# Loads of q, k and v in pieces of two pairs, tail groups inside one PSUM tile, the last output in two halves, and a new instruction order: a linear-attention and channel-mix kernel

## Chip, cores, metric

One core of a Trainium2 chip. The metric is device time in microseconds (us). The kernel is tuned already: every engine's instruction stream is written out by hand in one long list of words, and each engine works its own words off in that order. The question is what a change of loads, buffers and order does to it.

## The reference

```python
def phi(x):                                   # x: (8, 8, 576, 64), w_phi: (64, 128)
    proj = np.einsum('bhsd,df->bhsf', x, w_phi)
    proj = proj - np.max(np.abs(proj), axis=-1, keepdims=True)
    return np.concatenate([np.exp(proj), np.exp(-proj)], axis=-1)
q_p, k_p = phi(q), phi(k)
kv = np.einsum('bhsf,bhsd->bhfd', k_p, v);  z = np.sum(k_p, axis=2)
attn = einsum('bhsf,bhfd->bhsd', q_p, kv) / (einsum('bhsf,bhf->bhs', q_p, z)[..., None] + 1e-06)
x = attn.transpose(0, 2, 1, 3).reshape(8, 576, 512)
x_prev = x shifted by one position
xk = mu_k * x + (1 - mu_k) * x_prev;   xr = mu_r * x + (1 - mu_r) * x_prev
k = np.maximum(xk @ w_k, 0.0)                 # 512 -> 1024
out = sigmoid(xr @ w_r) * (k * k @ w_v)       # 1024 -> 512
```

Eight batches, each of 8 heads taken as 4 pairs (32 pairs n = 0 to 31). Each pair's 576 positions are 512 (the main part) and 64 (the "tail"). The tails of a batch are worked as a group. Then come two matmul stages of the feed-forward part per batch, on the tiles named ps_h, ps_r and ps_v.

## The kernel before

The order is a list of words. `name:slot` gives the PSUM slot, `/ENGINE` the engine, `+n@s` dummy matmuls that fill a wait, `.d` the end of a transfer. A number without a dot is a pair, `4.0` is batch 4 from its pair 0 on, `7.2` batch 7 from its pair 2 on: `lk7.2` loads k there, `mh18` splits the maxima of pair 18. An excerpt at pair 7 of 31, with five loads in a row:

```text
mt7:1 mc7/ACT lk3.0 lq3.0 lv3.0 lk4.0 lq4.0 rq8 lk4.0.d:0 kc6/ACT r0.1:0 th0.1 ka7 ea7 eb7 ...
```

A load is one transfer per tensor and batch (1152 KB in fp32, cast on the way to 576 KB in bf16; the sizes below, as in the profile, are those in bf16), issued by POOL. From batch 2 on there is one for all four pairs:

```python
def ld(which):
    def f():
        t = get(nat, b, inp, [128, NP, 2 * X], BF, "nat")
        src, o = ((k, 0), (q, X))[which]
        nc.gpsimd.dma_start(out=t[:, a0:a1, o:o + X], in_=heads(src, b, a0, a1))
    return f
def ldv():
    t = get(vt, b, inp, [128, NP, X], BF, "vt")
    nc.gpsimd.dma_start(out=t[:, a0:a1, :], in_=heads(v, b, a0, a1))
...
lparts = {b: [(0, NP)] for b in range(B)}
lparts[0] = [(0, 1), (1, 2), (2, 4)]
lparts[1] = [(0, 2), (2, 4)]
```

PSUM is used as three tiles of two banks (`P0` to `P2`) and two of one bank (`M0`, `M1`). A tail group takes one P tile and, one after the other, two M tiles:

```python
def tp():    # projections of the tails: k in bank 0, q in bank 1 (for its maxima)
    s["ps"] = ps = ptile(A, "ps_e")
    ...
def mhe():   # maxima split in two bf16 parts, on POOL
    ... nc.gpsimd.tensor_copy(...); nc.gpsimd.tensor_tensor(..., op=ALU.subtract)
def mte():   # transpose of the maxima
    s["pm"] = pm = motile(("mo", "m" + tag), "ps_me")
    nc.tensor.transpose(pm[:, 0:64].bitcast(BF), mh, ident)
def kae():   # subtracts the maxima from k's half: bank 0 of ps_e
def ekt():   # two exponentials on ACT that read bank 0 of ps_e (tiles tk0, tk1)
def qte():   # q again, transposed and less its maxima
    s["pq"] = ps = motile(("mo", "q" + tag), "ps_qe")
def eqe():   # two exponentials on ACT that read ps_qe (tiles tq)
```

The query exponentials of a pair, and the mix of x with its neighbour:

```python
def eq(pn):
    t = s[f"q{pn}"] = mid.tile([128, 2, 512], BF, name=f"q{pn}", bufs=BUFS["qpn"])
    for h in range(2):
        nc.scalar.activation(t[:, h, :]..., s["qT"]...[:, h], AF.Exp, scale=...)
def mix(i):                # xk, xr: one DVE instruction each
    nc.vector.scalar_tensor_tensor(out=t[...], in0=s["d"], scalar=mu[:, a:a + 1],
                                   in1=xs[:, a, 0:S], op0=ALU.mult, op1=ALU.add)
def mhx():                 # split of a pair's maxima, on POOL: tiles mhl
BUFS = {... "kpn": 2, "qpn": 2, "krelu": 3, "rt": 3, "kvs": 2, "d": 2, ...}
```

Of the kernel before, what the change touches and what calls it, by code (L numbers as in the profile page):

```python
# [19 lines left out]
ones ident lv0.0 lv0.0.d:0 lk0.1 lq0.1 lv0.1 dve2 hk hq hk.d:0 lk0.1.d:0 dve3 hq.d:0 lk0.0.d/ACT  # L20
lq0.0.d/DVE lk0.2 lq0.2 pt0:2+9@0 wphi wphi.d:0 mus dve1 lv0.2 lk1.0 pb0/DVE pa0/ACT tr0 tp0.0:2+1@0
rt0.0 mhe0.0 lk0.2.d:0 qp0:1 rq0 lq0.2.d:0 kp0:0 rk0 mte0.0:1+3@0 lq1.0 lq1.0.d:0 lv1.0 mh0
lq0.1.d:0 pt1:1 pa1/DVE mce0.0/ACT kae0.0 lk1.2 lq1.2 lv1.2 pb1/ACT tr1 lq1.2.d:0 qp1:1+2@0 mt0:1
rq1 ekt0.0 mc0/ACT wk.0 pt2:2 ka0 pb2/DVE pa2/ACT kp1:1 rk1 mh1 ea0 pt3:2 pb3/ACT lk1.0.d:0 eb0
pa3/DVE tr3 mt1:1+4@0 mc1/DVE tr2 vc0/POOL wk.1 qp2:2 ka1 ea1 mus.d:0 eb1 rq2 kv0:0 kc0/DVE wr.0
wk.1.d:0 wr.1 lv1.2.d:0 kp2:2+1@0 rk2 wv.0 qt0:0 pt4:1+1@0 lv1.0.d:0 mh2 mt2:1+1@0 qa0 qb0 lk1.2.d:0
pa4/DVE pb4/DVE qte0.0:0 eqe0.0 tp0.1:1 mc2/DVE ka2 tr4 lv0.2.d:0 pt5:0 ea2 rt0.1 mhe0.1
mte0.1:0+1@1 pb5/DVE wv.0.d:0 pa5/DVE eb2 mce0.1/DVE kae0.1+2@1 lv0.1.d:0 ekt0.1 pt6:0 pb6/ACT
pa6/DVE pt7:2 pa7/DVE nd0:1 qt1:0 rd0 pb7/ACT vc1/POOL vc2/POOL vc3/ACT qp3:2 rq3 kp3:1+1@1 wv.1 rk3
mh3 tr6 qa1 qb1 tp0.2:2+3@1 qte0.1:0 tr7 eqe0.1 rt0.2 mhe0.2 kv1:0 kc1/ACT xt0:1 xf0/ACT mt3:0  # L30
mc3/ACT nd1:0 tr5 vc4/POOL xe0/ACT ka3 ea3 eb3 df0/POOL mte0.2:1+1@0 rd1 xt1:0 mce0.2/DVE kae0.2
ekt0.2 tp1.0:0 qte0.2:1 eqe0.2 rt1.0 qp4:1 qt2:2 lk2.0 qa2 qb2 mhe1.0 mte1.0:1 rq4 xa0 kv2:1 kc2/ACT
mce1.0/DVE kae1.0 ekt1.0 vc5/POOL xf1/DVE xb0 qte1.0:1 wr.0.d:0 kp4:2 kv3:1 eqe1.0 kc3/ACT nd2:0 rk4
mh4 mt4:1 rd2 qp5:1 mc4/ACT ka4 rq5 xe1/ACT wk.0.d:0 ea4 eb4 lq2.0 xt2:1 lq2.0.d:0 qp6:0 rq6
df1/POOL xa1 qt3:1+1@0 qa3 kv4:2+1@0 kc4/DVE wk.d xb1 wr.1.d:0 kp5:0 qt4:2+1@0 rk5 qb3 nd3:1 rd3 mh5
xe2/ACT mt5:0+3@0 lk2.0.d:0 tr2.0 xf2/ACT xt3:1 qa4 qb4 mc5/ACT df2/DVE ka5 xe3/ACT xf3/ACT tr2.2
xa2 xb2 wv.1.d:0 ea5 eb5 nd4:2 rd4 df3/POOL xa3 qt5:1 qa5 xb3 kv5:0+3@0 tr2.2.d:0 kp6:2 xt4:1
xf4/ACT xe4/DVE kc5/ACT h0.0:0 h0.1:1 qb5 rl0.0/ACT rl0.1/ACT sq0.0/ACT vc6/POOL vc7/DVE rk6 qp7:1
nd5:0 df4/POOL rq7 mh6 mt6:1 mc6/ACT h0.2:0 rl0.2/ACT qt6:1 qa6 xa4 tr2.0.d:0 wr.d r0.0:1 tr9 xb4
sq0.2/POOL th0.0 tr8 rd5 h0.3:0 qb6 sq0.1/POOL rl0.3/DVE lv2.0 lv2.0.d:0 xt5:1 xf5/DVE xe5/DVE ka6  # L40
kp7:0 h0.4:0 h0.5:1 qp8:1 ea6 df5/POOL eb6 rl0.4/ACT sq0.4/ACT rk7 mh7 sq0.3/ACT kv6:2 rl0.5/DVE
mt7:1 mc7/ACT lk3.0 lq3.0 lv3.0 lk4.0 lq4.0 rq8 lk4.0.d:0 kc6/ACT r0.1:0 th0.1 ka7 ea7 eb7 tr11 tr10
lq3.0.d:0 tp2.0:1 rt2.0 h0.6:1 r0.2:0 rl0.6/DVE sq0.6/ACT th0.2 nd6:2 rd6 h0.7:1 mhe2.0 mte2.0:0
mce2.0/DVE vc8/POOL vc9/POOL kv7:0 kc7/DVE rl0.7/ACT vc10/POOL kae2.0 ekt2.0 qp9:2 rq9 qte2.0:1
xt6:0 sq0.7/POOL qt7:0 lk3.0.d:0 xf6/DVE xe6/DVE eqe2.0 qa7 qb7 kp8:1 rk8 kp9:2 rk9 wv.d sq0.5/POOL
v0.0:0 ob0.0 tr3.0 so0.0 mh8 mt8:1 nd7:0 mc8/ACT ka8 mh9 mt9:0 mc9/ACT xa5 tr3.2 xb5 v0.1:1 rd7
ob0.1 tr3.2.d:0 vc11/ACT ea8 df6/POOL eb8 xa6 xb6 v0.2:0 ob0.2 xt7:1 xe7/ACT xf7/ACT qt8:1 qa8 qb8
df7/DVE xa7 xb7 ka9 lv3.0.d:0 vc12/POOL kv8:0 r0.3:0 tr3.0.d:0 tr13 tr12 lq4.0.d:0 th0.3 v0.3:1
kc8/DVE ob0.3 kp10:0 so0.1 qp10:1 rq10 rk10 ea9 eb9 h1.0:0 h1.1:1 rl1.0/ACT sq1.0/ACT nd8:1 rd8
kv9:2 kc9/ACT h1.2:0 qt9:1 qp11:2 mh10 rq11 rl1.1/ACT xz8 rl1.2/ACT sq1.2/POOL mt10:1 so0.2 mc10/ACT  # L50
sq1.1/POOL h1.3:0 rl1.3/DVE qa9 qb9 r1.0:1 th1.0 sq1.3/POOL kp11:2 rk11 mh11 ka10 ea10 h1.4:0 tr15
eb10 lv4.0 rl1.4/DVE sq1.4/ACT h1.5:1 rl1.5/DVE mt11:0 mc11/DVE so0.3 nd9:1 qp12:0 sq1.5/ACT ka11
xz8.d:0 ea11 eb11 h1.6:0 h1.7:1 vc13/POOL vc14/POOL tr14 vc15/POOL rd9 rq12 xz9 qt10:1 xz9.d:0
rl1.7/DVE rl1.6/DVE lk5.0 kv10:2 kc10/DVE tp3.0:0 sq1.7/POOL rt3.0 qa10 mhe3.0 qb10 r1.1:1 th1.1
he0.0:0 rle0.0/DVE nd10:1 r1.2:1 sq1.6/ACT mte3.0:0 mce3.0/ACT rd10 xz10 xz10.d:0 qt11:2 th1.2
kp12:1 xu8/POOL df8/DVE xa8 so0.0.d:0 kae3.0 xu9/POOL qa11 qb11 rk12 v1.0:1 ob1.0 mh12 ekt3.0
he0.1:0 mt12:1 mc12/ACT xb8 kv11:2 lv4.0.d:0 so0.1.d:0 tr4.0 df9/DVE rle0.1/ACT kc11/ACT qp13:0
qte3.0:1 sqe0.0/DVE eqe3.0 xu10/POOL df10/POOL ka12 kp13:2 so0.2.d:0 so0.3.d:0 so1.0 ea12 so1.0.d:0
r1.3:0 eb12 rq13 rk13 nd11:0 rd11 th1.3 v1.1:1 xz11 xz11.d:0 mh13 sqe0.1/ACT xa9 xb9 ob1.1 xa10 xb10
mt13:0 mc13/ACT kv12:0 kc12/ACT ka13 ea13 eb13 qt12:1 qa12 tr4.0.d:0 tr16 vc16/POOL xu11/POOL  # L60
df11/POOL qp14:0 rq14 v1.2:1 ob1.2 qb12 re0:0 the0 kp14:0 rk14 xa11 kv13:2 kc13/DVE so1.1 qt13:1
mh14 xb11 v1.3:0 tr4.2 tr4.2.d:0 tr19 vc17/POOL ob1.3 so1.3 mt14:1 qa13 nd12:2 qb13 mc14/ACT
vc18/POOL qp15:1 rq15 ka14 so1.1.d:0 ea14 so1.2 eb14 lq5.0 rd12 xz12 xz12.d:0 h2.0:0 rl2.0/DVE ve0:1
qt14:2 lq5.0.d:0 obe0 soe0 soe0.d:0 kp15:0 kv14:1 sq2.0/ACT qa14 qb14 lv5.0 lv5.0.d:0 vc19/DVE
h2.1:1 rk15 kc14/ACT h2.2:0 nd13:2 rd13 xz13 xz13.d:0 lk6.0 rl2.1/ACT sq2.1/POOL mh15 rl2.2/ACT
sq2.2/POOL r2.0:1 th2.0 tr18 h2.3:0 so1.3.d:0 mt15:1 tr17 qp16:2 qp17:1 mc15/DVE rl2.3/ACT lq6.0
lv6.0 ka15 ea15 eb15 h2.4:0 h2.5:1 rq16 rq17 sq2.3/POOL rl2.4/ACT xu12/POOL df12/POOL qt15:2 qa15
tp4.0:0 kv15:1 kc15/ACT h2.6:0 sq2.4/ACT rl2.5/DVE rt4.0 mhe4.0 rl2.6/DVE nd14:1 rd14 h2.7:1 qb15
vc20/POOL xa12 sq2.5/POOL lk5.0.d:0 xu13/POOL mte4.0:0 kp16:2 rk16 mce4.0/ACT kp17:1 rk17 kae4.0
mh16 rl2.7/ACT ekt4.0 r2.1:0 r2.2:1 th2.1 mt16:0 mc16/DVE xb12 xz14 df13/DVE nd15:0 so1.2.d:0 rd15  # L70
sq2.6/ACT xz15 sq2.7/ACT lq6.0.d:0 th2.2 mh17 ka16 ea16 xa13 v2.0:0 ob2.0 xb13 tr5.0 tr5.2 tr5.0.d:0
tr20 v2.1:1 eb16 mt17:0 mc17/ACT xz14.d:0 kv16:2 kc16/ACT ob2.1 vc21/POOL vc22/POOL qp18:0 rq18 ka17
ea17 qte4.0:1 xu14/POOL eb17 kp18:2 rk18 v2.2:0 eqe4.0 tr5.2.d:0 tr23 qp19:1 lk6.0.d:0 xz15.d:0
xu15/POOL df14/POOL xa14 qt16:0 qa16 ob2.2 r2.3:1 th2.3 mh18 v2.3:0 rq19 qb16 df15/POOL mt18:1
mc18/ACT kv17:1 so2.0 kc17/ACT xb14 ka18 ea18 eb18 qt17:0 qa17 qb17 nd16:1 xa15 xb15 h3.0:1 ob2.3
rd16 xz16 h3.1:0 rl3.0/DVE sq3.0/POOL so2.3 qp20:1 kp19:2 h3.2:1 rl3.2/ACT so2.2 rl3.1/DVE rk19
so2.2.d:0 r3.0:0 rq20 h3.3:1 th3.0 mh19 sq3.1/ACT sq3.2/POOL vc23/ACT rl3.3/ACT mt19:0 mc19/DVE
nd17:1 r3.1:0 th3.1 sq3.3/ACT so2.0.d:0 tr22 qt18:0 rd17 xz17 xz17.d:0 xz16.d:0 xu16/POOL qa18 qb18
ka19 ea19 df16/POOL xa16 kv18:1 kc18/DVE h3.4:0 rl3.4/DVE lk7.0 tr21 tp5.0:1 rt5.0 h3.5:1 sq3.4/DVE
rl3.5/ACT h3.6:0 rl3.6/DVE eb19 nd18:0 rd18 h3.7:1 mhe5.0 mte5.0:0 xz18 rl3.7/DVE sq3.5/ACT qt19:2  # L80
qp21:0 xu17/POOL rq21 mce5.0/ACT kae5.0 ekt5.0 sq3.6/POOL df17/POOL r3.2:1 th3.2 qte5.0:0 kv19:1
lv6.0.d:0 eqe5.0 kc19/ACT kp20:0 so2.3.d:0 xb16 he1.0:1 sq3.7/DVE v3.0:0 so2.1 xz18.d:0 so2.1.d:0
tr6.0 rk20 mh20 rle1.0/DVE qa19 qb19 xu18/POOL df18/POOL vc24/POOL mt20:1 mc20/DVE kp21:2 ka20
vc25/POOL ob3.0 so3.0 rk21 mh21 he1.1:1 rle1.1/DVE nd19:1 r3.3:0 rd19 xz19 xz19.d:0 mt21:1 ea20 eb20
xa18 qt20:0 mc21/ACT th3.3 qp22:1 xb18 qa20 lq7.0 rq22 ka21 v3.1:0 v3.2:1 ob3.1 kv20:1 qb20 xa17
xb17 ea21 eb21 so3.0.d:0 kc20/ACT ob3.2 so3.2 qt21:2 kv21:0 kp22:1 tr6.2 so3.1 re1:1 tr6.2.d:0
xu19/POOL df19/DVE xa19 sqe1.0/ACT xb19 tr27 rk22 mh22 v3.3:0 ob3.3 kc21/ACT nd20:0 rd20 sqe1.1/POOL
xz20 qa21 qb21 nd21:2 mt22:0 the1 tr6.0.d:0 h4.0:1 tr24 mc22/ACT ka22 ea22 rd21 qt22:0 so3.2.d:0
qa22 rl4.0/DVE ve1:0 eb22 vc26/POOL sq4.0/DVE lv7.0 r4.0:1 th4.0 tr25 obe1 qb22 so3.3 qp23:2 rq23
vc27/POOL xz21 kp23:1 rk23 h4.1:0 rl4.1/ACT xz20.d:0 h4.2:1 rl4.2/ACT h4.3:0 qp24:0 kv22:2 xz21.d:0  # L90
# [67 lines left out]
def kernel(  # L158
# [17 lines left out]
    nc = tc.nc  # L176
# [351 lines left out]



    XPE = 8
    xkt, xrt = {}, {}

    def add_pair(n):
# [437 lines left out]
```

## Time and profile before

| | before |
|---|---|
| median of 3 runs (later, with the changed kernel, 4 runs) | 305.72 us (305.18) |
| lowest to highest | 304.64 to 307.18 us |
| profiled execution | 304.2 us |
| TensorE busy / idle | 278.4 / 25.8 us |
| first ps_h matmul (end of the start) | 51.9 us |
| DVE, ACT, POOL busy | 240.3, 223.3, 127.4 us |

The prediction below shows the lines behind most of this. Two more are needed for the comparison. The first, from the slices of the page, is the clock that TensorE was granted, in tenths of full speed, in 40 equal slices (9 is 0.9 or more); the second, from the groups, holds the query exponentials: line, engine, operation, tiles, shapes, count, then busy time and the mean of one in ns, then the idle time before them.

```profile
PEclk9999989999999999998999999999999999999999
...
L620 ACT ACTIVATE q<-ps_qT 128x512 bf16<-128x512 f32 x128 | 67.1, 622 | 3.0 <-PE ps_qT L612 2.8
```

Of 40 slices of 7.6 us the sixth and the nineteenth (137 to 144 us) show a clock below 0.9, the latter right behind the stalled transpose that the prediction dissects.

### The profile page before, as it was taken

The page shows a single profiled execution, that of the slowest core. Times are in us where ns is not written, and L with a number is a line of the kernel's source. Part 1 is how long each engine was busy: PE and PEld are TensorE (multiplying, and loading weights), DVE is VectorE, ACT ScalarE, POOL GpSimd, SP SyncE. Part 2 cuts the span into 40 slices and gives each one's busy share as a digit, 9 for nine tenths or more (in the row PEclk, how much of TensorE's full clock was granted, in tenths as well). Part 3 has the DMA queues.
Part 4 walks back from the last instruction along what each step waited for, and adds up shares of the span by engine and source line. Part 5 has one row for each costly group of instructions (what it writes and reads, how often), then busy time and mean ns, then how long its engine had stood idle before and what let it go on. Part 6 is the DMA issues. An engine that isn't in the chain of part 4 may idle for free.

```text
span 304.2 us, 9054 instructions
## 1 busy us (share of the span) xinstructions
PE 278.4 (92%) x3765; PEld 158.4 (52%) x3813; DVE 240.3 (79%) x369; ACT 223.3 (73%) x408; POOL 127.4 (42%) x261
## 2 busy tenths in 40 slices
PE   6688798999899999969999997999999999999993
PEld 2456465565456655534555654454556655554541
DVE  5776789979978999667978988799869888777331
ACT  3397899998689897855888884898797878923410
POOL 7763533696047346653443714353034403400400
PEclk9999989999999999998999999999999999999999
DMA  8999957399989957996957898913924364233125
GB/s 152 204 209 207 169 83 105 59 194 206 194 174 128 148 124 131 197 200 113 177 110 107 145 125 157 162 47 61 187 60 69 11 93 94 58 74 71 39 58 116
DMA packets 66137, 38.18 MB, mean 126 GB/s; under 512 B 47024, under 2 KB 60720, under 8 KB 66096
## 3 DMA queue, kind: packets, MB, share of 16 engines
q1 hardware_dynamic: 51280, 20.82, 39.4%
q0 software_dynamic: 14672, 16.48, 35.1%
q8 instruction: 30, 0.49, 0.7%
q10 hardware_dynamic: 144, 0.29, 0.3%
q14 instruction: 11, 0.09, 0.1%
HBM read 33.62 MB, written 9.44 MB: 142 GB/s over the span
## 4 chain that ended last, share of the span: by engine, by line
PE 61%; DVE 18%; DMA 7%; ACT 6%; issue 3%; POOL 2%; SPq 1%; DVEq 0%; POOLq 0%
PE ps_v L812 14%; PE ps_h L779 13%; PE ps_r L798 7%; PE ps_nd L656 5%; DMA xs<-x_sc 4%; PE ps_kv L635 4%; DVE nm L565 4%; DVE nm L560 3%; DVE xk L706 2%; PE ps_ve L896 2%; ACT q L620 2%; PE ps_he L866 2%; DVE xr L706 2%; PE ps_q L548 2%; PE ps_k L598 2%
## 5 line engine op out<-in xcount | busy, mean ns | idle before, releaser
L620 ACT ACTIVATE q<-ps_qT 128x512 bf16<-128x512 f32 x128 | 67.1, 622 | 3.0 <-PE ps_qT L612 2.8
L575 ACT ACTIVATE k<-ps_k 128x1024 bf16<-128x1024 f32 x64 | 62.9, 1038 | 5.6 <-PE ps_k L598 4.3
L779 PE MATMUL ps_h<-xk,wk_bf 128*128 128x512 bf16 x237 | 60.8, 379 | 1.3 <-issue 0.3
L812 PE MATMUL ps_v<-wv_bf,kk 128*128 128x512 bf16 x243 | 58.2, 379 | 1.0 <-issue 0.3
L565 DVE TENSOR_REDUCE nm<-ps_q 128x8 f32<-128x1024 f32 x32 | 38.7, 1218 | 4.3 <-PE ps_q L548 4.1
L560 DVE TENSOR_REDUCE nm<-ps_k 128x8 f32<-128x1024 f32 x32 | 38.8, 1217 | 3.8 <-PE ps_k L548 3.8
L812 PEld LDWEIGHTS <-kk 128*128 128x128 bf16 x256 | 23.9, 98 | 28.8 <-issue 1.9
L211 POOL TENSOR_TENSOR kk<-krelu 128x512 bf16<-128x512 bf16 x23 | 23.9, 1047 | 35.4 <-DVE krelu L205 21.7
L779 PEld LDWEIGHTS <-wk_bf 128*128 128x128 bf16 x256 | 22.5, 97 | 25.2 <-issue 2.3
L584 POOL CAST mhl<-nm 128x16 bf16<-128x16 f32 x32 | 8.0, 250 | 64.1 <-DVE nm L560 64.0
L798 PE MATMUL ps_r<-wr_bf,xr 128*128 128x512 bf16 x118 | 32.9, 394 | 1.2 <-issue 0.5
L804 ACT ACTIVATE rt<-ps_r 128x512 bf16<-128x512 f32 x32 | 19.5, 609 | 18.0 <-PE ps_r L798 15.7
L700 POOL TENSOR_TENSOR diff<-xs 128x576 bf16<-128x576 bf16 x21 | 28.0, 1336 | 7.6 <-DVE xs L682 2.8
L203 ACT ACTIVATE krelu<-ps_h 128x512 bf16<-128x512 f32 x39 | 23.2, 611 | 10.1 <-PE ps_h L779 8.3
L706 DVE SCALAR_TENSOR_TENSOR xk<-diff,mu_k_t,xs 128x576 bf16<-128x576 bf16 x32 | 28.5, 892 | 1.3 <-POOL diff L700 1.0
L818 DVE SCALAR_TENSOR_TENSOR ob<-rt,ps_v 128x512 f32<-128x512 bf16 x32 | 21.8, 682 | 8.7 <-PE ps_v L812 4.2
L666 DVE TENSOR_TENSOR x_sc<-ps_nd,rden 128x640 bf16<-128x640 f32 x32 | 26.4, 825 | 1.1
L706 DVE SCALAR_TENSOR_TENSOR xr<-diff,mu_r_t,xs 128x576 bf16<-128x576 bf16 x32 | 26.9, 840 | 0.0
L548 PEld LDWEIGHTS <-qkT 64*128 64x128 bf16 x512 | 17.6, 94 | 12.0 <-issue 9.7
L635 PE MATMUL ps_kv<-v,k 64*128 64x65 bf16 x1024 | 22.8, 192 | 0.6 <-ACT q L620 0.4
L635 PEld LDWEIGHTS <-k 64*128 64x128 bf16 x1024 | 19.9, 95 | 5.1 <-issue 3.8
L205 DVE TENSOR_SCALAR krelu<-ps_h 128x512 bf16<-128x512 f32 x25 | 17.1, 688 | 6.6 <-PE ps_h L779 6.0
(99 smaller groups left out, 467.5 us busy)
## 6 DMA issues: line engine op xcount, KB each, us to landing
out_dram<-ob SPq DMA_DIRECT2D x72, 128.0 KB, 2.4
nat<-in_k_dram POOLq DMA_DIRECT2D x6, 576.0 KB, 8.6
nat<-in_q_dram POOLq DMA_DIRECT2D x6, 576.0 KB, 8.9
vt<-in_v_dram POOLq DMA_DIRECT2D x6, 576.0 KB, 9.6
wk_bf<-in_moe_w_k_dram POOLq DMA_DIRECT2D x2, 512.0 KB, 10.8
wv_bf<-in_moe_w_v_dram POOLq DMA_DIRECT2D x2, 512.0 KB, 12.3
nat<-in_k_dram POOLq DMA_DIRECT2D x3, 288.0 KB, 7.4
nat<-in_q_dram POOLq DMA_DIRECT2D x3, 288.0 KB, 7.3
```

The costliest lines, as they stand in the source:

```text
L211: (nc.vector if eng == "DVE" else nc.gpsimd).tensor_tensor(out_, in_, in_, op=ALU.mult)
L560: nc.vector.tensor_reduce(s["nm"][:, 0, :], s["k"].rearrange("p a (g f) -> p (a g) f", f=128), axis=AX.X, op=ALU.max, apply_absolute_value ...
L565: nc.vector.tensor_reduce(s["nm"][:, 1, :], s["q"].rearrange("p a (g f) -> p (a g) f", f=128), axis=AX.X, op=ALU.max, apply_absolute_value ...
L575: nc.scalar.activation(s[f"k{pn}"], s["k"].rearrange("p a (g f) -> p (a g) f", f=128), AF.Exp, scale=(1.0 if pn == 0 else -1.0))
L620: nc.scalar.activation(t[:, h, :].rearrange("f (g a p) -> f g a p", g=4, a=2), s["qT"].rearrange("f a (g h p) -> f h g a p", g=4, h=2)[:, ...
L635: nc.tensor.matmul(ps[:, hh, pn * 65:(pn + 1) * 65], lhsT=s[f"k{pn}"][r, c, :], rhs=vb[r, a, 2 * g + par, :], start=(pn == 0 and c == 0), ...
L666: nc.vector.tensor_tensor(s["x"].rearrange("p (b s) d -> p b s d", b=2), ndv[:, :, :, 0:64], s["rd"].to_broadcast([128, 2, 5, 64]), op=ALU ...
L700: (nc.vector if eng == "DVE" else nc.gpsimd).tensor_tensor(s["d"], xs[:, a, 64:64 + S], xs[:, a, 0:S], op=ALU.subtract)
L706: nc.vector.scalar_tensor_tensor(out=t[:, a, (b % 2) * S:(b % 2 + 1) * S], in0=s["d"], scalar=mu[:, a:a + 1], in1=xs[:, a, 0:S], op0=ALU.m ...
L779: nc.tensor.matmul(ps, lhsT=wk_bf[:, c, fc * 128:(fc + 1) * 128], rhs=xkt[bp][:, c, m0:m0 + 512], start=(c == 0), stop=(c == NDC - 1))
L798: nc.tensor.matmul(ps, lhsT=xrt[bp][:, c, m0 + ci * 128:m0 + (ci + 1) * 128], rhs=wr_bf[:, c, :], start=(c == 0), stop=(c == NDC - 1))
L812: nc.tensor.matmul(ps, lhsT=s["kk"][:, fc, ci * 128:(ci + 1) * 128], rhs=wv_bf[:, fc, :], start=(fc == 0), stop=(fc == NFC - 1))
```

## The change

Its intent: let q, k, v arrive in smaller pieces spread over the program so that a piece never blocks the queues for long; free the two one-bank PSUM slots from the tail groups; give the tightest buffers a third copy; finish the last output sooner. The order of all words is new, and with it the engine of many instructions. The core of the diff (the list of words and the bookkeeping are cut):

```diff
-    BUFS = {... "kpn": 2, "qpn": 2, "krelu": 3, "rt": 3, "kvs": 2, "d": 2 ...}
+    BUFS = {... "kpn": 3, "qpn": 3, "krelu": 4, "rt": 4, "kvs": 3, "d": 3 ...}
-    lparts = {b: [(0, NP)] for b in range(B)}
+    lparts = {b: [(0, 2), (2, 4)] for b in range(B)}
 def mhe(eng):                                  # and mhx(eng): POOL or DVE by the word
-    nc.gpsimd.tensor_copy(mh[:, o:o + n], s["m"][:, c, 0:n])
+    pick(eng).tensor_copy(mh[:, o:o + n], s["m"][:, c, 0:n])
 def mte():
-    s["pm"] = pm = motile(("mo", "m" + tag), "ps_me")
-    nc.tensor.transpose(pm[:, 0:64].bitcast(BF), mh, ident)
+    nc.tensor.transpose(s["ps"][:, 1, 0:64].bitcast(BF), mh, ident)
 def qte():
-    s["pq"] = ps = motile(("mo", "q" + tag), "ps_qe")
+    s["pq"] = ps = s["ps"][:, 1, :]            # bank 1 of the tile whose bank 0 ekt reads
 def eq(pn):
-    for h in range(2):
-        nc.scalar.activation(t[:, h, :]..., AF.Exp)          # 128x512, twice
+    nc.scalar.activation(t.rearrange(...), s["qT"]..., AF.Exp)   # 128x1024, once
 def mix(i):
+    if eng == "POOL":                          # 11 of 64 mixes
+        nc.gpsimd.tensor_scalar(md, s["d"], mu[:, a:a + 1], None, op0=ALU.mult)
+        nc.gpsimd.tensor_tensor(t[...], md, xs[:, a, 0:S], op=ALU.add)
+        return
 # last output: ps_ve, ob and the stores in two halves of 256 columns,
 # the second half's two stores on the queues of SP and ACT
```

An excerpt of the new order, at pair 17 to 19. Four loads stand in a row, and between the fourth (lq7.0) and the fifth (lv6.0) there is no work of POOL:

```text
... kc18/ACT tr5.2.d:0 tr21 xz17 lv5.2 lq6.2 lk7.0 lq7.0 vc20/ACT sq3.2/DVE rk19 lv6.0 sq3.1/POOL ...
```

## The prediction

> **What bounds the kernel now.** I read first the busy shares (section 1 of the page), then the busy time by stage, then the chain of waits in the stages that came out badly. The stages are cut at the first ps_h matmul of each batch, found in the timeline (51.9, 82.7, 117.4, 153.7, 187.8, 219.7, 250.9, 276.9 us).
>
> ```profile
> PE 278.4 (92%) x3765; PEld 158.4 (52%) x3813; DVE 240.3 (79%) x369; ACT 223.3 (73%) x408; POOL 127.4 (42%) x261
> ```
>
> TensorE is the bound: 278.4 of 304.2 us, which leaves 25.8 us of idle time to win. 12.0 us of the busy time are the dummy matmuls on "ones", which keep the clock up at the start and do no work. The stages, columns: stretch, length, busy PE, PEld, DVE, ACT, POOL with counts, clock, DMA share, GB/s:
>
> ```profile
> 0.00:51.90 51.90, 40.50 (x673) 25.73 (x679) 38.86 (x75) 38.03 (x74) 28.60 (x64) 0.97 1.00 164
> 51.90:82.70 30.80, 29.38 (x383) 16.31 (x385) 27.39 (x40) 26.17 (x49) 17.67 (x29) 1.00 0.95 153
> 82.70:117.40 34.70, 34.12 (x546) 20.82 (x550) 31.45 (x45) 29.19 (x55) 16.88 (x36) 1.00 0.95 150
> 117.40:153.70 36.30, 32.95 (x440) 17.74 (x445) 28.45 (x38) 26.09 (x46) 18.33 (x36) 0.95 0.99 163
> 153.70:187.80 34.10, 32.10 (x474) 18.83 (x480) 29.28 (x42) 26.80 (x49) 13.60 (x31) 1.00 0.83 132
> 187.80:219.70 31.90, 30.60 (x391) 16.30 (x398) 28.73 (x42) 26.34 (x49) 12.43 (x27) 1.00 0.64 115
> 219.70:250.90 31.20, 30.94 (x473) 18.34 (x474) 25.66 (x42) 25.59 (x46) 10.01 (x21) 1.00 0.40 57
> ...
> 276.90:304.20 27.30, 22.23 (x123) 10.70 (x123) 9.06 (x16) 7.71 (x13) 3.18 (x3) 0.97 0.36 77
> ```
>
> TensorE idles 11.4 us before the first feed-forward matmul (and fills 12 us more with dummies), 3.4 us in the stage from 117.4 us, 5.1 us at the end, and 6.0 us in all the rest. The stage from 117.4 us has DMA full and a granted clock of 0.95. Its chain of waits shows why:
>
> ```profile
> 123.70 1.03 POOL kk L211
> 124.73 0.16 POOL mhl L584
> 124.89 0.07 issue
> 124.96 0.14 POOL mhl L585
> 125.10 13.39 DMA xs<-x_sc
> 138.49 0.05 issue
> 138.55 0.23 POOL xs L199
> ```
>
> A transpose of x by DMA took 13.4 us; after 150 us the median of the same kind is 2.9 us. In the window from 112 to 142 us five loads of 576 KB were issued by POOL (two of q, two of v, one of k, all between 117.5 and 127 us), and they landed after 11 to 16 us. POOL waits in order, so its small pieces mhlt and mhl for the next matmuls stood behind the copy that waits for the transpose: TensorE then waited 2.4 us on mhlt.
>
> **What the Trainium skill says.** "DMA: Bandwidth & Descriptors", section "Issuing engines are not separate DMA queues": transfers started by different engines run on the same 16 DMA engines and interleave; a second issuing queue saves only the sequencer's issue time. The trace agrees with the first half: the transposes from SP lengthen from 2.9 to 13.4 us when POOL's loads are in flight. "TensorE: Matmul & The Clock Gate", part 1: an idle TensorE has its clock gated and needs some 3.4 us of work to get it back. The trace agrees in kind: the clock in the stalled stage is 0.95, so a stall costs more than its idle time. "ScalarE: Activation LUTs", section "What ACT_TABLE_LOAD costs": 186 ns plus 0.833 ns per column for an activation with immediate scale, back-to-back ones overlapping by some 93 ns. The trace agrees: 128x1024 takes 1038 ns, 128x512 takes 622 ns. "GPSIMD Engine Reference", section "Key points": about half of VectorE's elementwise speed, on shared SBUF ports. Trace: the subtraction diff takes 1336 ns on POOL, 495 ns on DVE.
>
> **The change part by part.**
>
> *Query exponentials* (in the diff, not in its title). 128 activations of 128x512, 67.1 us busy, become 64 of 128x1024; the 64 key exponentials of that shape are 62.9 us. So 4.2 us less on ACT. The new assignments give more back: relu +8 x 0.6, square +10 x 0.64, copies of v +8 x 0.68, moving PSUM copies and the rest about -1: ACT goes from 223 to about 233 us. DVE loses 8 relus (0.69), 6 squares (0.55) and 11 mixes (0.87) and gains 18 small splits of maxima (about 0.25) and 6 of tails (0.5): about 231 us. POOL gets 18 more load issues (0.74 each, 13 us) and 11 mixes of two passes in fp32 (estimate 2.3 us each from the 1336 ns of diff, 25 us), loses 18 + 6 splits, 4 squares, 8 copies of v: about 142 us. None of the three becomes the bound; TensorE's real work stays the same (the matmuls are the same but for the last output, 38 fills for 39). So all gain must come out of idle time.
>
> *Start.* q and k now come before v. Before, ahead of the last q and k of batch 1 stand 0.58 MB (first pair, fp32) and 2.88 MB of pieces; after, 0.58 + 2.30 MB. The trace moves 1.63 MB in the first 10 us and 206 GB/s in the next: (3.46 - 1.63)/0.206 + 10 = 18.9 us against 16.1 us, 2.8 us earlier. Also POOL stops issuing in the trace between 6.7 and 9.7 us, since its split of the tail maxima waits for DVE; the new order puts these splits on DVE during the start. Against that, the chain from 7 to 23 us is one of reductions on DVE (1.23 each) and copies on ACT and DVE, not of DMA; summed by the new order, with the trace's durations, DVE has about 37 us of work before the first ps_h against 40 and ACT 42 against 43. So part of the 2.8 us is hidden and part is won by the lighter engines: **-3 us**.
>
> *Spread pieces.* In the stage of batch 2 the new order issues six pieces of 288 KB, 1.7 MB in place of 2.9 MB, placed over some 12 us of TensorE's work rather than 9. The stage loses 3.35 us idle and 36.3 x 0.05 = 1.8 us by the clock; a normal stage idles about 0.8 us. So 4.3 us are to be had; I take most: **-3.5 us**.
>
> *Tail groups in their own PSUM tile, third buffers.* These take 20 tiles of some 250 off the two one-bank slots, and give q, k, kv and diff a third buffer. The stages from 153.7 to 219.7 us idle 3.3 us, with waits on ps_m for a slot that ob had yet to free (1.6 us). The tile of two banks is held longer for it. **-1 us**.
>
> *Last output in halves.* After the last matmul (299.2) come ob 0.69, two issues on SP 1.10, about 2.4 us to landing. Half an ob saves about 0.27 (half of 512 columns at the 0.69 us rate, less its fixed part), one issue on each of two queues saves 0.55; the landing is near the same. 16 matmuls of 256 columns for 8 of 512 stream the same columns, with 8 more weight loads of 98 ns that are nearly hidden. **-0.8 us**.
>
> *Costs.* POOL's extra 15 us contend with DVE (the mix xk averages 892 ns over the whole run, but 814 at the median after 150 us, where POOL is less busy), ACT has 10 us more, and a new order has new small stalls: **+0.5 us**.
>
> Sum: -3 - 3.5 - 1 - 0.8 + 0.5 = -7.8 us; 305.7 - 7.8 = **298 us**, 2.5% faster.
>
> **Rivals.** *The start is bound by its chain, and the stall moves.* If loads are not what delays the start, and the same bytes collide with other transposes (the new order issues six pieces almost together before batch 4's first mixes, and four before batch 2's), only the tail and a bit of the stall are won: 302 to 304 us. For it: total bytes are unchanged and DMA is at 0.95 to 1.00 for the first 150 us. Against: the window with five loads is the only one with such a stall. *ACT or DVE becomes the bound.* Stage 2 of the new order has about 36 us of work by my durations on PE, ACT and DVE alike; exponentials then set the pace and two or three us come back: 300 to 302 us. For it: 233 us on ACT. Against: in the trace such a stage (82.7 to 117.4) idles 0.6 us. *The start gains much more.* If POOL's stop and v first were what held everything, the first feed-forward matmul comes 6 us earlier, and all buffers help: 293 to 295 us. For it: 11.4 us idle plus 12 us of dummies there. Against: latency of the first pairs' chain is unchanged.
>
> **Range and chances.** The main case is 298, the first two rivals lie 2 to 6 us above, the third 3 to 5 below. So 293.5 to 302.5 us for 8 in 10. The 2% line is 299.6 us; the main case and the third rival lie under it. Faster 0.64, within 2% 0.33, slower 0.03 (only if a new stall as large as the old ones appears).
>
> **What would show it.** First ps_h near 49 us, not 52; no DMA transpose of x over some 8 us and POOL's wait for them (33.5 us now) down by a third or more; the clock at 1.0 in all slices between 52 and 290 us; TensorE idle near 18 us with about the same busy time; q as 64 activations near 1.04 us; ACT near 233, POOL above 140; from the last matmul to the end about 4.2 us in place of 5. I am wrong if the first ps_h stays at 52 us, if a stage between 52 and 277 us idles 3 us or more, or if TensorE waits on exponentials in many places.

## The result, and the profile after

A ratio here and below is the mean time of one kernel's fast runs over that of the kernel before in the same rounds, so it is not quite the ratio of the medians quoted. A "point" is 0.01 of this ratio. A run more than 1.5% above the fastest of its kernel does not count as fast; for a kernel whose runs scatter widely this leaves only its better ones, so its median is quoted beside the ratio.

| | before | after |
|---|---|---|
| median (4 runs each) | 305.18 us | 317.27 us |
| lowest to highest | 304.40 to 307.18 | 315.53 to 320.67 |
| ratio of fast runs, 95% interval | | 1.0367 (1.0285 to 1.0449) |
| profiled execution | 304.2 | 314.8 |
| TensorE idle | 25.8 | 32.7 |
| first ps_h | 51.9 | 53.6 |

The changed kernel is 3.7% slower; the predicted range was 293.5 to 302.5 us. From the page of the kernel after: the busy shares, and the granted clock by slice.

```profile
PE 282.1 (90%) x3771; PEld 160.0 (51%) x3820; DVE 243.9 (77%) x411; ACT 232.2 (74%) x363; POOL 149.4 (47%) x230
...
PEclk9999799999999999999999599999999999999999
```

ACT came out as counted (about 233 us). POOL and DVE did not: 149.4 us against about 142, and 243.9 us against about 231. The clock has a deep dip, a 5, in the 23rd slice of 7.87 us, so from 173 to 181 us. Stages of the kernel after, cut at the first ps_h of each batch as in the prediction (stretch, length, busy PE, PEld, DVE, ACT, POOL, clock, DMA share, GB/s), and the inside of the worst one:

```profile
0.00:53.60 53.60, 41.46 (x613) 25.45 (x621) 40.69 (x96) 36.31 (x62) 36.65 (x46) 0.97 1.07 179
...
121.20:151.90 30.70, 28.13 (x394) 15.17 (x397) 25.72 (x39) 23.18 (x36) 12.71 (x27) 1.00 1.00 153
151.90:193.80 41.90, 33.70 (x432) 18.96 (x437) 30.78 (x44) 29.82 (x46) 19.93 (x33) 0.92 0.80 126
...
160.00:180.00 20.00, 13.52 (x186) 7.64 (x181) 12.21 (x16) 11.37 (x18) 8.18 (x14) 0.85 0.73 98
```

TensorE idles 12.1 us in the start, 8.2 us in the stage from 151.9 us, and 12.4 us in all the rest. So one stage holds a quarter of the idle time, and the clock falls to 0.92 there. What happens in it is read from POOL's timeline (start, length, line, operation, tiles; in brackets the idle time before and what ended it):

```profile
143.65 0.68 POOL L210 COPY v<-vt 128x576 bf16<-128x576 bf16 x1
154.26 0.20 POOL L595 CAST mhl<-nm 128x16 bf16<-128x16 f32 x1 [9.92 <-DVE nm L571]
154.54 0.22 POOL L596 TENSOR_TENSOR mhl<-nm,mhl 128x16 bf16<-128x16 f32 x1
154.75 0.74 POOL L332 DMA_DIRECT2D vt<-in_v_dram  x1
...
157.62 0.75 POOL L332 DMA_DIRECT2D vt<-in_v_dram  x1
```

POOL stood 9.9 us before one small split (pair 18) that waits for DVE's maxima, and then issued five pieces within 3.6 us. The chain of waits of the same kernel (start, length, what) shows what the pieces did:

```profile
157.65 0.13 POOL vt L332
157.78 12.73 DMA xs<-x_sc
...
170.87 1.51 DVE diff L707
...
175.74 0.61 DVE krelu L216
176.35 0.04 issue
176.39 0.27 PE ps_m L600
```

A DMA transpose of x, issued by SP just then, took 12.7 us. DVE's subtraction waits for it, the relu behind it on DVE waits too, and TensorE waits for the relu's PSUM slot. It is the same stall as before (13.4 us) in another place. The waits of TensorE by releaser (total, times, longest) name it first, and a new kind second and sixth:

```profile
PE ps_m L600 <- DVE krelu L216: 7.3, 3, 6.4
PE ps_e L505 <- ACT tk L500: 4.1, 5, 1.4
...
PE ps_e L493 <- ACT tq L515: 1.2, 1, 1.2
```

L505 is qte, which now writes bank 1 of the tile; L500 is ekt, which reads bank 0. L493 is kae, bank 0, behind eqe's reading of bank 1. So work on one half of the tile waits for readers of the other.

Two parts are as predicted: the query exponentials, the first line of the groups below, and the end of the timeline (ob in halves). The other lines of the groups are the mixes of x on POOL and the splits of maxima on DVE:

```profile
L630 ACT ACTIVATE q<-ps_qT 128x1024 bf16<-128x1024 f32 x64 | 63.6, 1035 | 6.5 <-PE ps_qT L623 6.4
...
L715 POOL TENSOR_SCALAR md<-diff,mu_k_t 128x576 f32<-128x576 bf16 x6 | 10.4, 1727 | 5.2 <-DVE diff L707 4.8
L716 POOL TENSOR_TENSOR xk<-md,xs 128x576 bf16<-128x576 f32 x6 | 7.7, 1282 | 0.5
...
L595 DVE CAST mhl<-nm 128x16 bf16<-128x16 f32 x18 | 6.5, 364 | 0.6
...
L596 DVE TENSOR_TENSOR mhl<-nm,mhl 128x16 bf16<-128x16 f32 x18 | 6.2, 346 | 0.6
```

```profile
310.02 0.42 DVE L922 SCALAR_TENSOR_TENSOR ob<-rt,ps_ve 128x256 f32<-128x256 bf16 x1 [1.18 <-PE ps_ve L915]
...
310.83 0.42 DVE L922 SCALAR_TENSOR_TENSOR ob<-rt,ps_ve 128x256 f32<-128x256 bf16 x1 [0.39 <-PE ps_ve L915]
```

The last matmul ends at 310.8 us and the kernel at 314.8: 4.0 us, where it had been 5.0 (299.2 to 304.2). A mix on POOL takes 1.73 + 1.28 = 3.0 us; the prediction had estimated 2.3. A split of maxima on DVE is two instructions, 0.36 + 0.35 = 0.71 us; the prediction had counted 0.25 us, so its 18 splits are 12.7 us in place of 4.5.

### The profile page after: what moved, and what is told of

Read it like the earlier page. It is cut to its first block, busy times and chain, and to the rows that moved or that the text cites. A ratio compares the mean times of both kernels' runs of the same rounds, so it can differ in the third digit from the quotient of the medians.

```text
span 314.8 us, 9011 instructions
## 1 busy us (share of the span) xinstructions
PE 282.1 (90%) x3771; PEld 160.0 (51%) x3820; DVE 243.9 (77%) x411; ACT 232.2 (74%) x363; POOL 149.4 (47%) x230
## 4 chain that ended last, share of the span: by engine, by line
PE 63%; DVE 17%; DMA 8%; POOL 4%; ACT 4%; issue 3%; POOLq 0%; ACTq 0%; DVEq 0%
PE ps_v L825 16%; PE ps_h L792 13%; PE ps_r L811 7%; DMA xs<-x_sc 6%; PE ps_nd L664 5%; DVE nm L571 4%; PE ps_kv L644 4%; DMA nat<-in_q_dram 2%; PE ps_qT L617 2%; PE ps_k L559 2%; PE ps_q L559 2%; DVE nm L576 2%; PE ps_he L879 2%; PE ps_ve L915 2%; PE ps_qT L623 2%
## 5 line engine op out<-in xcount | busy, mean ns | idle before, releaser
L630 ACT ACTIVATE q<-ps_qT 128x1024 bf16<-128x1024 f32 x64 | 63.6, 1035 | 6.5 <-PE ps_qT L623 6.4
L222 POOL TENSOR_TENSOR kk<-krelu 128x512 bf16<-128x512 bf16 x19 | 20.4, 1076 | 58.5 <-ACT krelu L214 58.4
L214 ACT ACTIVATE krelu<-ps_h 128x512 bf16<-128x512 f32 x47 | 28.1, 606 | 16.4 <-PE ps_h L792 15.6
L811 PE MATMUL ps_r<-wr_bf,xr 128*128 128x512 bf16 x114 | 31.2, 388 | 0.8 <-issue 0.2
L707 POOL TENSOR_TENSOR diff<-xs 128x576 bf16<-128x576 bf16 x19 | 24.6, 1294 | 2.5 <-ACT xs L208 1.6
L559 PEld LDWEIGHTS <-qkT 64*128 64x128 bf16 x512 | 17.7, 97 | 11.8 <-issue 7.2
L718 DVE SCALAR_TENSOR_TENSOR xk<-diff,mu_k_t,xs 128x576 bf16<-128x576 bf16 x26 | 22.4, 860 | 1.0 <-POOL diff L707 0.7
L210 POOL COPY xs<-xs 128x63 bf16<-128x63 bf16 x22 | 5.3, 244 | 36.0 <-DMA xs<-x_sc 36.0
L644 PE MATMUL ps_kv<-v,k 64*128 64x65 bf16 x1024 | 21.7, 190 | 0.8 <-ACT qkT L208 0.7
L718 DVE SCALAR_TENSOR_TENSOR xr<-diff,mu_r_t,xs 128x576 bf16<-128x576 bf16 x27 | 22.3, 827 | 0.0
L220 ACT ACTIVATE kk<-krelu 128x512 bf16<-128x512 bf16 x33 | 20.5, 635 | 2.3 <-DVE krelu L216 2.0
## 6 DMA issues: line engine op xcount, KB each, us to landing
wr_bf<-in_moe_w_r_dram POOLq DMA_DIRECT2D x2, 256.0 KB, 12.4
```

What stands on the lines that cost most here:

```text
L214: nc.scalar.activation(out_, in_, AF.Relu, scale=HALF)
L559: nc.tensor.matmul(ps[:, par, g * 128:(g + 1) * 128], lhsT=qkT[b][r, g0 + gg + g, :], rhs=wph[r, :], start=(g == 0), stop=(g == 3))
L630: nc.scalar.activation(t.rearrange("f j (a p) -> f j a p", a=2), s["qT"].rearrange("f a (j p) -> f j a p", p=64), AF.Exp, scale=(1.0 if pn ...
L644: nc.tensor.matmul(ps[:, hh, pn * 65:(pn + 1) * 65], lhsT=s[f"k{pn}"][r, c, :], rhs=vb[r, a, 2 * g + par, :], start=(pn == 0 and c == 0), ...
L718: nc.vector.scalar_tensor_tensor(out=t[:, a, (b % 2) * S:(b % 2 + 1) * S], in0=s["d"], scalar=mu[:, a:a + 1], in1=xs[:, a, 0:S], op0=ALU.m ...
L811: nc.tensor.matmul(ps, lhsT=xrt[bp][:, c, m0 + ci * 128:m0 + (ci + 1) * 128], rhs=wr_bf[:, c, :], start=(c == 0), stop=(c == NDC - 1))
```

## The experiments

Sixteen kernels ran, all with correct results. They take the change apart along these lines. **The old stall's logic** (the prediction's): fewer bytes in flight beside a transpose are a gain. **Issue time**: each further load costs POOL's in-order time, whatever its bytes. **Shared tile**: the tail group's tile makes TensorE wait for exponentials. **Burst**: five pieces behind one wait remake the stall. **Mixes on POOL** and **the order itself** are the remaining suspects. "Old order" below means the order and engine choices of the kernel before, with the changed code.

The four calls, of four kernels each, had these medians of the kernel before: 306.31, 307.21, 306.78 and 307.34 us.

### e1: the changed code in the old order

```diff
-ORDER = (new)
+ORDER = (that of before, with the loads split in two adjacent words,
+         qte and eqe moved to directly behind ekt, the last output in halves)
```

qte had to move, since the P tile is taken by other work soon after; the place directly behind ekt was my choice, and e9 shows that it is a bad one.

> All code of the change (pieces of two pairs, tails in their own PSUM tile, one query exponential, third buffers, last output in halves), but the old order and the old engine choices; only the two halves of each load stand side by side and the second half of the tail groups follows the first at once. Theory A (the new order is what costs, by one burst of loads behind a blocked POOL): 302 to 306 us, no stage between the first feed-forward matmuls of batches 3 and 4 over 36 us. Theory B (the mixes and splits put on other engines cost): also 302 to 306. Theory C (the code itself costs: more loads that each wait for an older one to land, PSUM held longer by the tails): 312 us or more.

Measured: 325.58 us, ratio 1.0564 (1.0488 to 1.0639). The old order does not rescue the code; the code alone loses more than the whole change. The waits of TensorE in this kernel begin with

```profile
PE ps_e L501 <- ACT tk L496: 9.8, 9, 1.3
```

nine waits of 1.1 us, one for nearly each of the ten tail groups.

### e2, e3: the burst taken away in two ways

```diff
 # e2: in the new order
-xz17 lv5.2 lq6.2 lk7.0 lq7.0 vc20/ACT ... lv6.0 ... lk7.2 ... xu17/POOL ... xu19/POOL
+xz17 vc20/ACT ... xu17/POOL lv5.2 lq6.2 lv6.0 ... xu19/POOL lk7.0 lq7.0 lk7.2
 # e3: in the new order
-mh18/POOL
+mh18/DVE
```

> The changed kernel, but six loads (lv5.2, lq6.2, lv6.0, lk7.0, lq7.0, lk7.2) stand later on POOL: three after the shift xu17, three after xu19, so that none is in flight when the transposes xz16 and xz17 start. Nothing else moves. Theory A: those transposes land in 3 to 5 us instead of 11 to 13, the stage of batch 3 (41.9 us) falls to some 33 us, the whole to 307 to 310 us. Theories B and C: 314 us or more.

> The changed kernel with one word changed: the split of maxima mh18 runs on DVE instead of POOL. POOL then does not stand 9.9 us in front of the five loads; they leave some 10 us before the transposes. Theory A: the transposes land in 4 to 8 us, 308 to 313 us in all. Theories B and C, and also the view that the place of the loads in the program is what counts: 315 to 318 us.

Measured: e2 315.65 us (309.86 to 318.06), ratio 1.0193 (1.0100 to 1.0285), from two fast runs of four, so that it proves little by itself; e3 311.90 us (310.40 to 312.56), ratio 1.0180 (1.0126 to 1.0234). e3 is the clear one: 1.9 points better than the change. The stage that took 41.9 us takes 33.6 us in e2 and 35.6 in e3. e3 changes one word. POOL no longer stands before that split: two of the five loads go out at 147.3 and 148.0 us, the other three at 160.6 to 162.0, after a wait of 11.8 us for the transposes that free their buffer:

```profile
160.55 0.71 POOL L322 DMA_DIRECT2D nat<-in_k_dram  x1 [11.79 <-DMA qkT<-nat]
```

The transposes of x issued between 140 and 185 us land after 6.6 us at most, and the wait on the relu is no longer among the first of TensorE's. So it is the gathering of five, not these loads as such, that remade the stall. The burst is a cause in the changed kernel, worth about half of the loss when taken away alone; e11 below shows that this gain did not carry over.

### e4: the mixes back on DVE

```diff
-xa0/POOL  xb0/POOL  ...   (11 words)
+xa0/DVE   xb0/DVE   ...
```

> The changed kernel with the 11 mixes xa and xb that had gone to POOL back on DVE. Theory A: the burst stays, 314 to 318 us. Theory B (two fp32 passes on POOL, 3 us each, delay the chain and slow DVE on the shared ports): 306 to 311 us, first feed-forward matmul at 51 us or earlier.

Measured: 324.02 us, ratio 1.0602 (1.0539 to 1.0664): 2.3 points worse than the change, which neither theory had expected. The mixes on POOL help, at 3.0 us each; POOL's sheer busy time is not what costs.

### e5, e6, e7: pieces and shared tile, each alone and neither, in the old order

```diff
 # e5 = e1 with whole loads
-lparts = {b: [(0, 2), (2, 4)] for b in range(B)}
+lparts = {b: [(0, NP)] for b in range(B)}
 # e6 = e1 with the tails in M tiles and in their old places again
-s["pq"] = ps = s["ps"][:, 1, :]
+s["pq"] = ps = motile(("mo", "q" + tag), "ps_qe")      # and mte, mce the same
 # e7 = both
```

> As e1 (old order, 325.6 us), but every load of batches 2 to 7 in one piece again; tails stay in their own PSUM tile. Theory D: each load costs POOL 0.72 us to issue whatever its size, and 18 more of them stand in a row in front of the small splits that TensorE waits for; undoing them takes off 6 to 10 us, so 316 to 320 us. Theory E: nearly all of e1's loss is the tails' tile; then 322 to 326 us here. The burst theory alone (bytes in flight) expects no change either, since the bytes are the same: 323 to 327 us.

> As e1, but the tail groups have the two one-bank tiles of before again, with the order of before to the word; loads stay in pieces. Theory E (one tile for the tails makes TensorE wait for the exponentials that read its other bank, 9.8 us in nine waits in e1): 314 to 318 us. Theory D: most of the loss stays, 318 us or more.

> Old order, whole loads, tails in their own one-bank tiles; what is left of the change is one query exponential for two, the third buffers and the last output in halves. If pieces and tails are the two costs: 302 to 306 us, at or a little under the kernel before. If one of the other three parts costs: 308 us or more.

Measured, as ratios of fast runs (median in brackets):

| old order | tails in M tiles | tails in one tile |
|---|---|---|
| whole loads | e7: 0.9966, 0.9942 to 0.9990 (306.07) | e5: 1.0420, 1.0334 to 1.0506 (319.02) |
| pieces | e6: 1.0158, 1.0088 to 1.0228 (312.34) | e1: 1.0564, 1.0488 to 1.0639 (325.58) |

Pieces cost 1.9 points alone and 1.4 beside the shared tile; the shared tile (with qte where I put it) costs 4.5 and 4.1. The two nearly add up. e5 is where theory D had put it; e6 is below the ranges of both theories. What is left in e7, the merged query exponentials, the third buffers and the last output in halves, gains 0.3% (20 runs). That is 1 us, and the end of its profile is 0.4 us shorter than before (4.6 us from the last matmul, not 5.0), so little is left for the merged exponentials and the third buffers.

Where the pieces cost is plain from the stages: e6 and e7 differ mostly in the stage from the first to the second batch's ps_h, 30.7 us in e7 and 35.3 in e6; no other stage differs by more than 1.5 us. First e7's window over that stage (it begins 0.2 us before the first ps_h), then e6's:

```profile
51.90:82.80 30.90, 29.51 (x384) 16.42 (x389) 27.56 (x41) 25.94 (x42) 17.62 (x29) 1.00 0.94 150
```

```profile
51.10:86.40 35.30, 30.77 (x383) 17.04 (x385) 27.65 (x40) 26.09 (x42) 21.81 (x35) 0.95 0.93 153
```

POOL (last busy column before the clock) has 6 instructions and 4.2 us more, the stage is 4.6 us longer, TensorE idles 4.5 us in place of 1.4. The bytes per second are nearly the same (153 and 150 GB/s). The chain of waits of e6 there:

```profile
61.35 2.89 POOL nat L323 x4
64.24 1.44 POOL vt L328 x2
65.68 2.87 POOL nat L323 x4
68.55 0.21 POOL mhlt L477
...
69.49 0.23 PE ps_me L483
```

Ten issues of 0.72 us in a row, 7.2 us, and behind them the small split mhlt for which TensorE waits. In e7 the same five loads are five issues in 3.7 us.

### e8: qte beside kae in the new order

```diff
-kae1.0 ekt1.0 lk2.2.d:0 ... rk5 qte1.0 qt4:0 eqe1.0
+kae1.0 qte1.0 ekt1.0 lk2.2.d:0 ... rk5 qt4:0 eqe1.0     # so in all ten tail groups; in two it stood so already
```

Both writes to the tile now come ahead of both readings of it, so within a group no write has to wait for an exponential.

> The changed kernel with its new order, only that in each of the ten tail groups the two TensorE steps kae and qte stand together, ahead of the exponentials of both banks, so that neither waits for an exponential that reads the other bank. Theory E: the waits of TensorE on the exponentials tk and tq (5.3 us in seven) go, 311 to 314 us. If these waits are hidden by later ones: 316 to 318 us.

Measured: 311.33 us, ratio 1.0135 (1.0063 to 1.0208): 2.3 points better than the change. In its waits of TensorE, the two lines on tk and tq are gone; the burst's wait stays on top:

```profile
PE ps_m L595 <- DVE krelu L211: 8.3, 3, 7.1
PE ps_pt L339 <- DMA nat<-in_q_dram: 3.1, 2, 2.3
```

### e9: the same in the old order, whole loads

```diff
-kae1.0 ekt1.0 qte1.0:1 eqe1.0
+kae1.0 qte1.0:1 ekt1.0 eqe1.0       # e5, all ten groups
```

> As e5 (old order, whole loads, tails in one tile; ratio 1.042), only that in each tail group qte follows kae at once, ahead of the exponentials. Theory E (the tails' cost is the wait of TensorE for the exponentials that read the tile's other bank): back to e7, ratio 0.99 to 1.01. If the cost is that the two-bank slot is held longer: 1.03 or more.

Measured: 309.44 us (10 runs), ratio 1.0081 (1.0048 to 1.0115). Of the shared tile's 4.5 points, 3.4 were the place of qte; 1.1 remain against e7. So most of the tile's cost is the place of qte. For the rest e9's waits name a candidate: TensorE waits on the tail's query exponential (tq) 5.8 us in six waits, for other work (ps_k, ps_qT, ps_nd, ps_kv) that takes a P tile next, and never in e7. But the profiled execution of e9 is no longer than that of e7 (305.3 and 305.6 us), so this is not shown.

### e10, e11, e12: the new order with its defects undone

```diff
 # e10 = e8 with whole loads (lparts as in e5)
 # e11 = e8 with mh18/POOL -> mh18/DVE
 # e12 = e10 with mh18/POOL -> mh18/DVE
```

> As e8 (new order, tails' steps together; ratio 1.0135), with every load of batches 2 to 7 in one piece at the place of its first piece. Theory D (18 issues of 0.72 us on POOL): ratio 0.99 to 1.005, since in the old order the pieces cost 1.9%. If the new order hides the issues: 1.01 to 1.02; if whole loads make the burst before the transposes of batch 4 larger: above 1.02.

> As e8, with the split mh18 on DVE as in e3. If the stall by the burst and the tails' waits are two costs that add (e3 took 1.9% off, e8 2.3%): ratio 0.99 to 1.00. If taking away one only uncovers the other: 1.01 or more.

> As e11, with whole loads as in e10: all three suspected costs undone, the new order otherwise kept. If they add: ratio 0.97 to 0.99, faster than before. If the new order has nothing to give: 0.995 or more.

Measured:

| | median | lowest to highest | ratio of fast runs |
|---|---|---|---|
| e10 | 306.23 (4 runs) | 301.06 to 308.01 | 0.9857 (0.9759 to 0.9956) |
| e11 | 312.12 (20 runs) | 307.58 to 316.44 | 1.0117 (1.0082 to 1.0152) |
| e12 | 303.11 (4 runs) | 299.65 to 309.22 | 0.9781 (0.9703 to 0.9859) |

Whole loads against pieces are worth 2.8 points in the new order (e8 to e10) by fast runs, but e10 has only two; by the medians of all runs it is 1.5. So it is not shown that they are worth more here than in the old order, and it is not all issue time. In e10's profiled execution the burst's stall is gone as well, though mh18 is still on POOL and waits there:

```profile
149.05 0.20 POOL L588 CAST mhl<-nm 128x16 bf16<-128x16 f32 x1 [6.17 <-DVE nm L564]
...
154.29 0.79 POOL L320 DMA_DIRECT2D nat<-in_k_dram  x1 [4.75 <-DMA qkT<-nat]
```

The next three loads, whole ones of 1.7 MB together, waited 4.7 us more for their buffers and left when the transposes of x had been issued (150.8 to 153.4 us); these landed after 5.9 us at most, and the stage takes 33.4 us. The first ps_h comes at 51.1 us in e10 and 51.0 in e12, against 54.3 in e8 and 53.6 in e11. e12 is the best version; its class is "unclear" (neither clearly 2% faster nor clearly the same), because runs of these two kernels scatter by 2 to 3% and only two of four count as fast; the profiled run of e12 is not one of them. By the medians of all runs e12 is 1.2% faster than the kernel before (303.11 to 306.78), by fast runs 2.2%.

e11 is a miss. Taking the burst away (e3: 1.9 points) adds nothing that the runs show once qte stands right: 1.0117 against 1.0135. In the profiled execution the stage does shrink, 40.7 to 36.2 us, but the runs do not follow; that execution was among the fastest of 20, and 9 of them are too slow to count as fast. Why is open; so is the gain of e12 over e10, whose intervals overlap.

### e13: the second halves of five loads behind the split that waited

```diff
 # e6, old order
-lk3.0 lk3.2 lq3.0 lq3.2 lv3.0 lv3.2 lk4.0 lk4.2 lq4.0 lq4.2 ... mhe2.0/POOL
+lk3.0 lq3.0 lv3.0 lk4.0 lq4.0 ... mhe2.0/POOL lk3.2 lq3.2 lv3.2 lk4.2 lq4.2
```

If only the place of the issues ahead of mhlt mattered, this would bring nearly all of the cost back.

> As e6 (old order, tails in their own tiles, loads in pieces; ratio 1.0158), with the second halves of five loads (k, q, v of batch 3, k, q of batch 4) issued by POOL after the tail split mhe2.0 instead of before it. If the place in POOL's queue is the cost: ratio 0.995 to 1.005, and the stage from the first feed-forward matmul of batch 0 to that of batch 1 some 31 to 32 us instead of 35.3. If pieces cost wherever they stand: 1.012 or more.

Measured: 310.42 us (14 runs), ratio 1.0093 (1.0059 to 1.0126): 0.65 of the 1.9 points came back, between the two answers expected; the stage takes 33.9 us. The chain of waits shows the wait moved, not gone:

```profile
69.33 0.72 POOL vt L328
70.05 1.44 POOL nat L323 x2
71.49 1.88 POOL v L206 x3
73.37 2.00 POOL kk L218 x2
75.37 0.05 issue
75.41 1.40 PE ps_v L822 x3
```

Now three copies of v and two squares stand behind the issues, and TensorE waits for the squares. POOL's timeline has no gap from 60 to 78 us there; in this stretch the place of the issues chooses which wait it is.

### e14: eighteen loads that carry nearly nothing

```diff
 # e7 (whole loads, tails in M tiles), old order
+def tiny(t):
+    return lambda: nc.gpsimd.dma_start(out=t, in_=q[0, 0, 0:128, :])   # 16 KB, unused
 # one at each place where e6 has the second half of a load
```

> As e7 (old order, whole loads, own tail tiles; ratio 0.9966), with 18 useless loads of 16 KB each on POOL at the very places where e6 has the second halves; their data are never read. If the issue itself costs, whatever the bytes: ratio 1.01 to 1.02 like e6, each issue about 0.7 us on POOL. If the cost of the pieces lies in the bytes' order of landing: 0.995 to 1.003.

Measured: 311.88 us (14 runs), ratio 1.0141 (1.0103 to 1.0179), as e6 with its pieces. The groups of POOL by shape (count, busy time, mean ns): the 11 loads of v (six of them whole, five the pieces of batches 0 and 1), and the tiny ones.

```profile
L326 POOL DMA_DIRECT2D vt<-in_v_dram x11 | 8.2, 743 | 0.1
...
L437 POOL DMA_DIRECT2D tik<-in_q_dram x6 | 3.4, 566 | 0.0
L437 POOL DMA_DIRECT2D tiv<-in_q_dram x6 | 3.4, 564 | 0.0
```

The big loads are whole again and in their old places; only issues were added. The stage from the first to the second batch's ps_h takes 35.9 us, as in e6. So more issues are enough for the whole cost; neither the size of the pieces nor how their bytes lie in the DMA queues is needed for it. It is not POOL's busy time alone: in that stage mhlt comes some 4.5 us later than in e7, of which six tiny issues are 3.4 us, and 1.2 us is POOL standing once at an issue until an earlier load had landed.

### e15, e16: new order, whole loads, tails in M tiles

```diff
-s["pq"] = ps = s["ps"][:, 1, :]
+s["pq"] = ps = motile(("mo", "q" + tag), "ps_qe")     # slots chosen by me where one came free first
 # qte7.0, eqe7.0 moved behind mc29;  e16: mh18/DVE too
```

> The new order with whole loads and the tails in one-bank tiles of their own (e10 without the shared tile). If the shared tile costs 1.1% even with its steps together, as in the old order: ratio 0.97 to 0.98. If it costs nothing in the new order: 0.98 to 0.99, as e10. If e10 was a lucky draw: 0.995 or more.

> As e15, with mh18 on DVE. If the stall before batch 4 is then gone: 0.96 to 0.975 and no stage over 36 us but that of batch 1 and batch 5, which hold more work in the new order. If e15 has no such stall: the same as e15 within 0.5%.

Measured: e15 324.36 us, ratio 1.0534 (1.0473 to 1.0596); e16 321.67 us, ratio 1.0409 (1.0344 to 1.0475). In the new order M tiles for the tails are much worse than the shared tile (e10: 0.9857). Both miss what was expected. In e15's waits, behind one on the relu as after the burst (5.8 us), other work stands for a slot that a tail's exponentials hold:

```profile
PE ps_v L819 <- ACT tq L509: 4.4, 3, 2.1
...
PE ps_m L594 <- ACT tq L509: 2.0, 1, 2.0
```

The new order was made for the shared tile and leaves no room in M0 and M1. The slots were my own choice, so the size of the loss is not that of the best possible placement. e16 is a fourth trial of mh18 on DVE: 1.25 points better than e15, after 1.9 (e3), 0.2 (e11) and 0.8 (e12).

## Why the prediction was wrong

Step by step, by its own terms.

**Start, -3: failed; +1.7 in the profile.** With the new order POOL stood 9.4 us in the first 54 us at load issues until an older transfer had landed (2.5, 1.8, 1.7 and 1.5 us are the largest entries); in the kernel before there is no such wait in that time. I had taken an earlier place in the list for an earlier start. The pieces have a share: with whole loads the same order reaches its first ps_h at 51.1 and 51.0 us (e10, e12), with pieces at 54.3 and 53.6 (e8, e11). But e10's POOL stands 7.7 us in the same way, so those waits alone do not make the difference, and the rest of its cause is open. The start also varies by itself: 54.6 us in e2 and 56.2 in e3, against 53.6 in the changed kernel with the same words up to there, so one profile of it proves little. Over all ten profiles of the new order the two groups do not overlap, though: 51.0 to 52.3 us with whole loads (e10, e12, e15, e16), 53.6 to 57.9 with pieces. In the old order they do.

**Spread pieces, -3.5: failed, and it is the step that names the error.** I read the 13.4 us transpose as too many bytes in flight and credited smaller, spread pieces with its removal. Two things were missed. First, "spread" is a property of the program, not of time: one wait of 9.9 us on POOL's queue gathered five pieces into 3.6 us, and a transpose of 12.7 us was there again, in the next stage (rival "the stall moves", which I gave 302 to 304 us). Second, I counted the issues, 18 x 0.74 = 13 us on POOL, and set them aside because none of the three helper engines became the bound. They stand in line ahead of splits, copies of v and squares that TensorE waits for. Measured in the old order: +1.9 points, some 5.9 us, for which e14 shows the issues to suffice; in the new order 2.8 points by fast runs, the burst's stall included. The sign that I had named went the wrong way: POOL's wait for the transposes, 33.5 us before, was to fall by a third and is 36.0 us.

**Tails in their own tile, -1: failed.** I saw the slots that it frees, and noted that the tile is held longer, but not that qte and ekt now touch one tile, and that a write behind a read of it waits even where the banks differ. In the change this cost 2.3 points (after to e8), in the worst placement (e5, e1) 4.5 and 4.1. The sign condition I wrote, "if TensorE waits on exponentials in many places", is what happened: 5.3 us in six waits.

**Last output, -0.8: right.** 5.0 us became 4.0 (4.6 in e7).

**Query exponentials: right in size. Balance: right for ACT, not for DVE and POOL.** 64 x 1035 ns; ACT 232.2 (predicted about 233, though the terms listed sum to 234.7). DVE 243.9 where about 231 was counted (the terms listed sum to 229): the 18 splits account for 8 us of the miss. POOL 149.4 where about 142 was counted: the mixes take 34 us in place of 25 (the prediction quotes the skill for about half of DVE's speed on POOL; the figures that it sets beside this, 1336 and 495 ns, are a factor of 2.7). ACT and DVE did not become the bound: that rival fell, and e4 shows the mixes on POOL to be a help, though at 3.0 us each rather than 2.3.

**Costs, +0.5: mis-sized.** Its terms were contention and small stalls; none of the three costs above is in it.

The sum by experiments, from after to e12: qte beside kae, -2.3 points; whole loads, -2.8; the split of pair 18 on DVE, -0.8 and not significant. That is 1.0367 to 0.9781. By the medians of all runs the steps are -2.6, -1.5 and -1.0, from 1.040 to 0.988. They are not three separate causes, since whole loads (e10) took the burst's stall away too. The new order itself is good: with the same whole loads and qte beside kae it has 0.9857, the old one 1.0081. So a gain lay in the order, near the predicted size by fast runs (2.2 points) and less by medians (1.0), and two of the parts that I had credited with gains spent more than that.

What stays open: why e11 gains nothing where e3 gains 1.9 points; whether the wait for P tiles makes the shared tile's last 1.1 points in the old order; why POOL's issues in the start wait for landings, and how the pieces delay it; and whether e12 is really over 2% faster.

## What to carry to other kernels

Before a load is split, count its issues and look at what stands behind them in the issuing engine's queue, in the stretch where that engine has no gap; its average busy share does not show it. Where two steps share a tile, put all writes ahead of the first reader, or give them two tiles. And where transfers are "spread" by program order, look for the long wait ahead of them in the same queue: it gathers them into a burst.

## What the Trainium skill lacked or had wrong

- "DMA: Bandwidth & Descriptors", section "Issuing engines are not separate DMA queues", calls the time to initiate a DMA usually small beside the DMA. That holds here, 0.7 us beside 7 to 10 us to landing, and yet the issues cost: each takes POOL 0.71 to 0.79 us for 288 to 576 KB and 0.55 to 0.57 us for 16 KB, and 18 more of them lengthen a kernel of 306 us by 1.4 to 1.9% in the old order. The section doesn't say that the other work of the issuing engine stands behind it.
- "Perfetto Trace Analysis", section "DMA Optimizations", says that splitting DMAs may let some start sooner where the DMA engines are generally idle. The condition did not hold here (DMA share 0.95 to 1.00 in the first 150 us), and splitting lost 1.9 points alone; a word on the issuer's time belongs beside that advice. The item after it speaks of the issuer only where descriptor generation is the bottleneck, and here POOL was busy 42 to 47%.
- No page says that, in a program such as this one, a write to one bank of a tile waits for readers of its other bank: 9.8 us in nine waits in e5, none in e9, which differs in order alone. These are waits that the program sets; no run shows whether the hardware needs them.
